# A planned attention and two-layer kernel: the order planned anew, k and q of the first batch loaded and turned in another form, two buffers for finished rows

## Chip, core and metric

The kernel runs on one core of one Trainium2 chip. Times are microseconds of the device, from a profile of one execution or as the median of several timed runs. Less is better.

## The reference

Attention with a threshold, then two feed-forward layers over the same 2304 rows. Everything is float32 at the inputs except the layers' weights, which arrive as float64 and are read as pairs of 32-bit words.

```python
# q, k, v: (4, 8, 576, 64); tau = 0.02
scores = q @ k.T / 8
scores = where(scores >= max(scores) - tau, scores, -1e9)
attn = softmax(scores) @ v                      # per batch and head
x = attn -> (2304, 512)
x = relu(x @ w_in) ** 2 @ w_out                 # 512 -> 2048 -> 512
h = x @ w2_in
out = (h * tanh(softplus(h))) @ w2_out          # 512 -> 2048 -> 512
```

## The kernel before

**Work.** Heads are taken in pairs, four pairs a batch, 16 pairs in all. The rows of a batch are five tiles (four of 128 and a tail of 64); a unit of attention is two heads with one tile of query rows. The 2304 rows form nine blocks of 256 for the layers; blocks 2b and 2b+1 need batch b, block 8 the tails of all batches. Each block of the first layer has eight steps (`first_part`): two products into PSUM `h`, a square on ScalarE, a split into a high and a low float32r half, two products into `acc`. A block's x is read back from DRAM in four pieces `xl`, turned on TensorE into a place `s0` or `s1` and split (`x_first`). The second layer (`second`) follows the same way, four quarters a block.

**Two kinds of attention.** Batch 0 (`kinds="dddd"`) is direct: `job_direct` loads k and q as float32 with `natural`, turns them on TensorE (`turn`), and scores are float32 products; the attention weights are turned on TensorE too (`values_direct`), the products with v are in `turned`. The three other batches (`job`) scale and split k, q and the attention weights into 16-bit halves, turn them by a transposing transfer on SyncE's queue (`transpose`) and use 16-bit products. Both have on VectorE a maximum (`top`) and a mask (`mask`) for each head and tile, on ScalarE the exponential. The finished rows of a pair are normalized on VectorE into `xs` (`normal`) and stored to `x_dr`.

**Weights.** `weights` loads a half tile of 512 KB into a raw place, turns the words into a float32 on ScalarE and VectorE, and splits it. In the beginning the places of weights not yet needed serve as extra buffers: `PAR["ex"]` says how many of the 16 go to raw weights (`cr`), work tiles (`cw`), raw k and q (`raw`), turned attention weights (`pd`) and scores (`sc`).

**Order.** Nothing is ordered by hand. Every operation is an `Op` with a time for each engine that may do it, its dependences and a due time. `Plan.forwards` lets each engine take, of what is ready, the one due first; `Plan.backwards` then makes due times out of the schedule from its end, and both are repeated `fbi` times. `BIAS` shifts the choice between engines. `stay` lets TensorE prefer a product of the same type (16-bit or not) if it is due little later than the first. The instructions are issued in the order that comes out, and each engine, SyncE's queue of transfers too, works through its own strictly in that order. A transfer's time in the plan is one shared queue (`dma_free`), its size over a fixed rate, and a fixed landing time.

Of the kernel before, what the change touches and what calls it, by code (L numbers as in the profile page):

```python
# [29 lines left out]
    on="S",  # L30
    da=1.0,
    cd=(-62.495, -1.335, 25.036),
    urg=-0.838,
    rawt=3.181,
    kinds="dddd",
    cgen=28.773,
# [3 lines left out]
    tb2=251.89,  # L40
    down2=-35.293,
    sp=(2, 0),
    off=(28.102, 71.229, 105.592, -167.157, 71.05, 36.991, -15.061, -2.604),
    ahead=(12.281, 2.776, 12.775, 8.713, 23.761, 22.36, 4.666, 4.666, 49.594, 49.594),
    ts=[0.85, 1.2, 0.45, 0.65],
    start=-23.978,
    area={"sc": ["x0", "x1"], "hl": ["x2"]},
    jobahead=20.215,
    fbi=6,
    stay=0.742,  # L50
    kinds2="ssss",
    tv=1.3,
# [19 lines left out]
class Op:  # L72
    __slots__ = ("opts", "fn", "deps", "due", "xfer", "n_dma", "tab", "two", "half", "start", "end", "eng", "n")


class Plan:
# [6 lines left out]
    BIAS = {"V": 2.018, "A": -4.391, "P": 2.61, "S": 0.46}  # L83
    HIDE = 0.3
    LAND = 1.9
# [14 lines left out]
    def op(self, opts, fn, r=(), w=(), x=(), due=0.0, xfer=None, n_dma=1, tab=None, two=False, half=False):  # L100
# [3 lines left out]
        o.opts, o.fn, o.due, o.xfer, o.tab, o.n, o.n_dma = opts, fn, due, xfer, tab, len(self.ops), n_dma  # L104
# [41 lines left out]
    @staticmethod  # L146
    def lag(p, e):

        if p.xfer is not None:
            return 0.97  # L150
        if p.eng == e:
            return 0.0 if e == "T" else 0.17
        return 0.27 if e == "T" else 0.2 if p.eng == "T" else 0.16

    def backwards(self, succ):
# [8 lines left out]
        def offer(o):  # L164
            t = 0.0
            for z in succ[o.n]:
                t = max(t, done[z] + self.lag(o, ops[z].eng))
            if o.xfer is not None:
                t += self.LAND + o.xfer
            cand[o.eng][o.n] = t  # L170
# [4 lines left out]
        for _ in ops:  # L175
# [10 lines left out]
            free[e] = done[n] = t + (0.57 * o.n_dma if o.xfer is not None else o.end - o.start)  # L186
# [8 lines left out]
    def forwards(self, succ):  # L195
# [3 lines left out]
        free = dict.fromkeys(engs, 0.0)  # L199
        cand = {e: {} for e in engs}  # L200
        dma_free = gen_free = port = 0.0
# [15 lines left out]
        while count < len(ops):  # L217
            best = None
            for e in engs:
# [3 lines left out]
                t = max(free[e], min(c.values()))  # L223
                now = sorted((ops[n].due, n) for n, at in c.items() if at <= t)
                pick = None
                for _, n in now:
                    o = ops[n]
                    if len(o.opts) > 1:
# [3 lines left out]
                        for a, d in o.opts.items():  # L232
                            if a != e:
                                ahead = sum(
                                    min(ops[m].opts.values()) for m, at in cand[a].items()
# [8 lines left out]
                if pick is None:  # L244

                    later = [at for at in c.values() if at > t]
                    nxt = min((f for f in free.values() if f > t), default=None)
                    stop = min(later + ([nxt] if nxt is not None else []), default=None)
                    if stop is None:
                        continue  # L250
                    free[e] = max(free[e], stop)
# [22 lines left out]
            if o.xfer is None and (e == "P" or e == "V" and o.two):  # L274
# [10 lines left out]
            if o.xfer is not None:  # L285
# [8 lines left out]
            else:  # L294
                o.end = free[e]
# [9 lines left out]
def attention_moe_moe_kernel(ctx: ExitStack, tc: tile.TileContext, q, k, v, tau, w1i, w1o, w2i, w2o, out):  # L305
# [63 lines left out]
    def dma(fn, r=(), w=(), x=(), due=0.0, mb=0.1, n=1, on=PAR["on"]):  # L369

        cost = {"S": 0.57 * n, "A": PAR["da"] * n, "P": 1.05 * n}
        op({e: cost[e] for e in on}, lambda e: fn({"S": nc.sync, "A": nc.scalar, "P": nc.gpsimd}[e]), r, w, x, due,
           xfer=0.05 * n + mb / 0.36, n_dma=n)

    def transpose(dst, src, r, w, due):
        op({"S": 1.36}, lambda e: nc.sync.dma_start_transpose(out=dst(), in_=src()), r, w, due=due, xfer=1.0)
# [29 lines left out]
    op({"S": 0.5}, consts, w=[K], due=-50.0, xfer=1.5)  # L406
# [4 lines left out]
    def weights(layer, kind, j, due, places, wplaces):  # L411
# [5 lines left out]
        for half in range(2):  # L417
# [63 lines left out]
            dma(load, w=[raw], due=due - 12, mb=0.52)  # L481
# [40 lines left out]
    for kind, n in zip(("cw", "cr", "raw", "pd", "sc", "f", "nat", "e", "hl", "pt"), PAR["ex"]):  # L522
# [51 lines left out]
    def split(raw, sc, cb, dst, hi, lo, due, n):  # L574
        def h(e):
# [22 lines left out]
    def job_v(p, due):  # L598
# [16 lines left out]
        dma(load_v, w=[rv], due=due - 12, mb=0.4, n=3)  # L615
# [6 lines left out]
    def natural(e, raw, x, twice):  # L622

        for h in range(2):
            e.dma_start(out=raw[:, 0:4, h, :], in_=x[h, 0:512, :].rearrange("(p j) d -> p j d", j=4))
        for a in range(1 + twice):
            e.dma_start(out=raw[64 * a:64 * a + 64, 4], in_=x[:, 512:576, :].rearrange("h p d -> p h d"))

    def job(p, due):
# [5 lines left out]
        for raw, x, z in ((rk, kk, 16), (rq, qq, 15)):  # L635
            dma(lambda e, raw=raw, x=x: natural(e, raw().rearrange("p j (h d) -> p j h d", h=2), x, 1),
                w=[raw], due=due - z, mb=0.36, n=4)
# [25 lines left out]
    def job_direct(p, due):  # L663

        p.c, p.cv = K, None
        p.KT, p.QT = sbuf(rot("KT0", "KT1"), [128, 576], F32), sbuf(rot("Q0", "Q1"), [128, 576], F32)
# [660 lines left out]
```

## Time and profile before

| | |
|---|---|
| median of 3 timed runs | 1073.74 us (1072.82 to 1074.63) |
| the profiled execution, its own time | 1072.09 us |
| its span on the core | 1070.3 us |
| mean granted TensorE clock | 0.985 |
| TensorE busy | 1013.1 us, 95% |
| VectorE, ScalarE, GpSimd busy | 749.4, 795.2, 40.0 us |

The span is the time from the first to the last instruction of the program. PE is TensorE's products, PEld its weight loads, DVE VectorE, ACT ScalarE, POOL GpSimd, SPq SyncE's queue of transfers. An instruction's row ends in square brackets with the idle time of its engine before it and with what ended this. Names such as `wo5h` or `wi4h` in the first 100 us are weight places lent to other tiles.

### The profile page before, as it was taken

Reading aid. Unit: us, or ns where it says so; the run is one execution under the profiler, and the core shown is the slowest. Engines: PE = TensorE matmul, PEld = TensorE weight load, DVE = VectorE, ACT = ScalarE, POOL = GpSimd, SP = SyncE. Lnnn points to the kernel's source line nnn. Section 1 sums busy time; section 2 is a strip of 40 time slices with the busy share of each in tenths; the row PEclk is TensorE's granted clock in tenths of the full one; section 3 lists DMA queues with packets and bytes.
Section 4 is the critical chain, followed back from the end, with each engine's and each line's share of the span. In section 5 each row is a group of like instructions: output and inputs, shape, how many; then the busy total and the mean of one; then the engine's idle time right before and its main releaser. Section 6 shows DMA issues by size and latency. Waiting matters only on the chain. (4 is left out here: it accounts for less than half of the span.)

```text
span 1070.3 us, 23743 instructions
## 1 busy us (share of the span) xinstructions
PE 1013.1 (95%) x9364; PEld 914.4 (85%) x9364; DVE 749.4 (70%) x1768; ACT 795.2 (74%) x1309; POOL 40.0 (4%) x38
## 2 busy tenths in 40 slices
PE   6887889889999999999999999999999999999998
PEld 4565588778889888889899999989999999999997
DVE  5889999989898988887867128975544554454453
ACT  6799799777776877676678449988766777676684
POOL 1231003000000000000000000000000000000000
PEclk9999889999999999999999999999999999999999
DMA  9645446898997898976676105511001000010000
GB/s 254 180 121 149 121 124 131 157 171 168 172 164 122 155 178 170 162 148 127 115 207 215 57 2 159 157 60 41 20 21 40 21 21 20 21 40 20 1 20 21
DMA packets 246416, 113.75 MB, mean 106 GB/s; under 512 B 211104, under 2 KB 228000, under 8 KB 246304
## 3 DMA queue, kind: packets, MB, share of 16 engines
q1 hardware_dynamic: 246016, 111.71, 46.6%
q8 instruction: 73, 1.20, 0.5%
q10 hardware_dynamic: 288, 0.52, 0.1%
q14 instruction: 39, 0.32, 0.1%
HBM read 58.33 MB, written 14.16 MB: 68 GB/s over the span
## 5 line engine op out<-in xcount | busy, mean ns | idle before, releaser
L379 PE MATMUL s<-KT,area 64*128 64x64 f16 (+6 forms) x880 | 90.9, 327 | 6.5 <-ACT area L684 2.6
L766 ACT ACTIVATE e<-area,m 128x576 f32<-128x576 f32 x100 | 75.5, 767 | 22.0 <-DVE area L743 8.9
L1126 ACT ACT_TABLE_LOAD x70 | 89.8, 1283 | 1.2
L508 DVE TENSOR_TENSOR gl<-r,gh 128x512 fp32r<-128x512 f32 x87 | 59.9, 689 | 41.0 <-ACT gh L498 39.5
L743 DVE TENSOR_SCALAR_CACHE_REDUCE area<-s,c 128x576 f32<-128x576 f32 x100 | 79.4, 811 | 10.7 <-PE s L379 10.2
L777 DVE SCALAR_TENSOR_TENSOR e<-area,n,e 128x576 f32<-128x576 f32 x100 | 80.1, 812 | 6.2 <-ACT e L766 5.1
L806 DVE TENSOR_TENSOR hl<-e,hl 128x512 f16<-128x512 f32 (+1 forms) x142 | 64.3, 465 | 16.7 <-ACT hl L801 16.4
L379 PE MATMUL small<-V,pt 128*128 128x64 f16 (+1 forms) x1680 | 64.2, 194 | 8.5 <-DMA pt<-hl 6.9
L379 PEld LDWEIGHTS <-pt 128*128 128x128 f16 (+1 forms) x1680 | 54.4, 101 | 19.0 <-DMA pt<-hl 9.3
L1078 ACT ACTIVATE r<-h 128x512 f32<-128x512 f32 x72 | 42.8, 594 | 36.7 <-PE h L379 30.2
L801 ACT ACTIVATE hl<-e 128x576 f16<-128x576 f32 x74 | 50.2, 680 | 25.9 <-DMA pt<-hl 13.8
L498 ACT ACTIVATE gh<-r 128x512 fp32r<-128x512 f32 x90 | 56.6, 629 | 16.2 <-PE acc L379 13.6
L1174 DVE TENSOR_SCALAR area<-area 128x512 f32<-128x512 f32 x37 | 15.7, 424 | 70.2 <-ACT area L1130 70.1
L1130 ACT ACTIVATE area<-area 128x512 f32<-128x512 f32 x74 | 46.3, 630 | 0.5
L508 DVE TENSOR_TENSOR gl<-e,gh 128x512 fp32r<-128x512 f32 x36 | 24.8, 689 | 30.9 <-ACT gh L498 30.8
L1085 ACT ACTIVATE r<-r 128x512 f32<-128x512 f32 x72 | 45.4, 630 | 1.2
L1130 ACT ACTIVATE area<-s 128x512 f32<-128x512 f32 x24 | 14.3, 597 | 39.8 <-PE s L379 39.6
L379 PEld LDWEIGHTS <-area 64*128 64x128 f16 (+1 forms) x720 | 24.5, 97 | 22.2 <-issue 3.8
L498 ACT ACTIVATE gh<-e 128x512 fp32r<-128x512 f32 x36 | 22.6, 628 | 26.6 <-PE acc L379 26.5
L379 PEld LDWEIGHTS s<-KT,area 64*128 64x128 f32 (+1 forms) x160 | 19.0, 211 | 19.8 <-issue 11.5
L457 ACT ACTIVATE area<-area 128x512 int32<-128x512 uint32 x44 | 35.2, 799 | 0.0
L1200 DVE TENSOR_TENSOR r<-s,area 128x512 f32<-128x512 f32 x23 | 15.9, 691 | 27.1 <-ACT area L1130 27.1
(755 smaller groups left out, 4042.7 us busy)
## 6 DMA issues: line engine op xcount, KB each, us to landing
area<-in_moe_w_in_dram SPq DMA_DIRECT2D x22, 512.0 KB, 4.3
area<-in_moe_w_out_dram SPq DMA_DIRECT2D x22, 512.0 KB, 4.2
xl<-xdr SPq DMA_DIRECT2D x36, 128.0 KB, 3.0
x2dr<-stg SPq DMA_DIRECT2D x18, 256.0 KB, 3.3
xdr<-xs SPq DMA_DIRECT2D x32, 128.0 KB, 2.5
f<-in_v_dram SPq DMA_DIRECT2D x12, 256.0 KB, 3.0
f<-in_k_dram SPq DMA_DIRECT2D x22, 128.0 KB, 3.3
area<-in_q_dram SPq DMA_DIRECT2D x20, 128.0 KB, 3.0
```

The source lines that it names most:

```text
L379: nc.tensor.matmul(o, l, r, start=start, stop=stop, skip_group_check=True)
L498: nc.scalar.activation(out=o, in_=i, func=AF.Copy)
L508: VEC[e].tensor_tensor(out=part(lo), in0=src(), in1=f32(part(hi)), op=ALU.subtract)
L743: nc.vector.tensor_scalar(out=sc(), in0=s()[:, 0:576], scalar1=c()[:, 3:4], scalar2=None, op0=ALU.mult, op1=ALU.min, accum_out=m()[:, i:i ...
L766: lambda e: nc.scalar.activation(out=ex(), in_=sc(), func=AF.Exp, bias=m()[:, i:i + 1], scale=-1.0),
L777: nc.vector.scalar_tensor_tensor(out=ex(), in0=sc(), scalar=nt()[:, i:i + 1], in1=ex(), op0=ALU.is_le, op1=ALU.mult, accum_out=l()[:, 0, u ...
L801: nc.scalar.activation(out=hl()[:, 0:576], in_=ex(), func=AF.Copy)
L806: VEC[e].tensor_tensor(out=hl()[:, a:a + n], in0=ex()[:, z:z + n], in1=hl()[:, z:z + n], op=ALU.subtract)
L1078: nc.scalar.activation(out=halves(r()), in_=turned_out(ph()), func=AF.Relu)
L1085: nc.scalar.activation(out=r(), in_=r(), func=AF.Square)
L1126: nc.scalar.preload_act_table_set({"ln": "natural_log_exp_and_others", "sig": "sigmoid_and_others"}[table])
L1130: nc.scalar.activation(out=out, in_=in_, func=func, **kw)
```

## The change

The planner gets a queue for each issuing engine, and for each kind of transfer four measured figures: issue time, the offsets of its pieces, and the time in the queue. Products' times are set anew, and with them all tuned numbers: due times of the blocks, offsets, biases, the shares of lent places (raw weights from six places to three, scores from one to three, raw k and q from five to six). `stay` becomes negative. In the direct batch k and q are loaded head by head with one transfer for four tiles and one for the tail, in pieces of 1 KB instead of 256 B; turning is ten products with the identity instead of five transposes. `natural` for the other batches changes the order of axes in the view, not the pieces. `xs` gets two places, `xl` two instead of three. `PAR["split"]` stays empty, so the code for a kept k and v is not used; `turns=("h",)` chooses the place as before.

```diff
 PAR = dict(
-    ex=(2, 6, 5, 2, 13, 6, 14, 11, 15, 29),     # cw cr raw pd sc ...
-    blk=[31.355, 90.417, 191.623, 253.139, 358.304, 447.476, 530.093, 674.428, 716.104],
-    fbi=6,
-    stay=0.742,
+    ex=dict(cw=2, cr=19, raw=6, pd=2, sc=3),
+    exo=("cw", "sc", "raw", "pd", "cr"),
+    blk=list((32.57, 96.77, 191.37, 255.65, 363.12, 471.61, 568.36, 741.61, 801.39)),   # digits cut
+    fbi=8,
+    stay=-6.225741638509871,
...
-    BIAS = {"V": 2.018, "A": -4.391, "P": 2.61, "S": 0.46}
+    BIAS = {"V": 2.2504733291199734, "A": -9.770909151037873, "P": 2.6062465814423676, "S": 0.46}
...
-            if o.xfer is not None:
-                if e == "P":
-                    go = free[e]
-                else:
-                    go = gen_free = max(t + 0.03, gen_free) + o.n_dma * 0.53
-                    free[e] = gen_free + (dur - 0.53 * o.n_dma if e == "S" else -self.HIDE)
-                done = max(go + self.LAND, dma_free) + o.xfer
-                dma_free = done
-                o.end = done
+            o.end = free[e]
+            if o.load is not None:
+                off, last, z = o.load
+                t += PAR["land"] + (dur - 0.6 if e == "P" else 0.0)
+                to = max(t, queue[e])
+                other = max(f for a, f in queue.items() if a != e)
+                z += min(z, max(0.0, other - to)) * self.SHARE
+                o.end = queue[e] = max(t + off + last, to + z)
...
+    LOADS = {
+        "n4": (2.5, 1.86, 0.19, 1.42), ... "n2": (1.2, 0.62, 0.19, 1.0),
+        "xs": (0.58, 0.0, 0.36, 0.36), ... "xl": (0.42, 0.0, 0.39, 0.39),
+        "x2": (0.42, 0.0, 0.63, 0.63), ... "turn": (1.32, 0.0, 1.14, 1.14),
+    }
...
     def job_direct(p, due):
-            raw = sbuf(rot(*spare["raw"]), [128, 5, 2, 64], F32)
-            dma(lambda e, raw=raw, x=src: natural(e, raw(), x, 0), w=[raw], due=due - 9 - z, mb=0.36, n=3)
+            raw = sbuf(rot(*spare["raw"]), [128, 2, 5, 64], F32)
+            def load(e, raw=raw, x=src, j0=j0, j1=j1, main=main):
+                e.dma_start(
+                    out=raw()[:, :, j0:main, :].rearrange("p h j d -> p h (j d)"),
+                    in_=x[:, 0:512, :].rearrange("h (p j) d -> p h j d", j=4)[:, :, j0:main, :].rearrange(
+                        "p h j d -> p h (j d)"
+                    ),
+                )
+                if j1 == 5:
+                    e.dma_start(out=raw()[0:64, :, 4, :], in_=x[:, 512:576, :].rearrange("h p d -> p h d"))
...
-                    nc.tensor.transpose(
-                        o()[:, 128 * j:128 * j + n], raw()[0:n, j].rearrange("p h d -> p (h d)"), ident[0:n, 0:n]
-                    )
-            op({"T": 0.74}, turn, r=[raw, K], w=[o], due=due - z)
+                    for h in range(2):
+                        mm(o()[64 * h:64 * h + 64, 128 * j:128 * j + n], raw()[0:n, h, j, :], ident[0:n, 0:n], True, True)
+            op({"T": 0.3 * (j1 - j0)}, turn, r=[raw, K], w=[o], due=due - z)
...
-        op({"T": PAR["ts"][direct] if hh < 2 else PAR["ts"][2 + direct]}, scores, ...
+        op({"T": (1.2 if direct else 0.93) if hh < 2 else 0.65 if direct else 0.5}, scores, ...
-            xs = sbuf("xs", [128, 2, 128], F32)
+            xs = sbuf(rot("xs0", "xs1"), [128, 2, 128], F32)
-        op({"T": 1.41}, fn, ...                                   # mlp_in; down the same
+        op({"T": 1.345}, fn, ...
-                xl = sbuf(rot("xl0", "xl1", "xl2"), [128, 256], F32)
+                xl = sbuf(rot("xl0", "xl1"), [128, 256], F32)
```

## Rows read from the trace of the kernel before

**Rows 1.** The page: busy time of each engine, and the granted clock in 40 slices.
```profile
PE 1013.1 (95%) x9364; PEld 914.4 (85%) x9364; DVE 749.4 (70%) x1768; ACT 795.2 (74%) x1309; POOL 40.0 (4%) x38
...
PEclk9999889999999999999999999999999999999999
```

**Rows 2.** Busy time by stage: stretch, its length, engines' busy us, clock, DMA, GB/s.
```profile
140.00:240.00 100.00, 89.51 (x1051) 79.42 (x1050) 95.53 (x248) 84.20 (x145) 9.33 (x8) 1.00 0.75 148
...
300.00:540.00 240.00, 232.65 (x2868) 210.13 (x2865) 203.78 (x589) 171.52 (x292) 4.71 (x4) 1.00 0.83 147
...
720.00:1070.00 350.00, 345.34 (x2348) 323.57 (x2346) 164.49 (x277) 247.64 (x360) 0.00 (x0) 1.00 0.07 23
```

**Rows 3.** Waits of TensorE, 54 to 540 us: us in total, times, longest.
```profile
PE small L379 <- DMA pt<-hl: 6.9, 13, 1.2
PE h L379 <- ACT xh L1045: 3.3, 2, 1.7
...
PE s L1033 <- DMA xl<-xdr: 2.7, 2, 1.7
...
PE small L379 <- DMA pt<-area: 0.2, 1, 0.2
PE small L844 <- ACT pt L902: 0.2, 1, 0.2
```

**Rows 4.** Timeline of the first 13 us: start, duration, instruction.
```profile
1.18 1.36 SPq L625 DMA_DIRECT2D wo5h<-in_k_dram  x2
...
4.57 0.63 SPq L627 DMA_DIRECT2D wo5l<-in_q_dram  x1
...
6.73 1.38 PE L676 MATMUL s<-ident,wo5l 128*128 128x128 f32 x5
...
9.44 0.66 ACT L449 ACTIVATE stg<-area 128x512 f32<-128x512 f32 x1 [2.09 <-DMA area<-in_moe_w_in_dram]
...
10.69 2.40 PE L379 MATMUL s<-KT,area 64*128 64x512 f32 x8 [2.58 <-ACT area L684]
...
12.41 0.47 SPq L698 DMA_DIRECT2D V<-in_v_dram  x1
...
12.92 0.88 SPq L702 DMA_DIRECT2D V<-in_v_dram  x1
```

**Rows 5.** Timelines of SyncE, VectorE and TensorE around 45 us.
```profile
41.41 8.06 SPq L940 DMA_DIRECT2D xdr<-xs  x2
...
48.46 0.42 DVE L917 TENSOR_TENSOR xs<-small,l 128x256 f32<-128x256 f32 x1 [4.17 <-DMA xdr<-xs]
...
48.94 0.47 PE L844 MATMUL small<-ident,e 128*128 128x128 f32 x1 [3.84 <-DVE xs L917]
...
53.50 2.18 PE L379 MATMUL s<-KT,area 64*128 64x512 f32 x8
```

**Rows 6.** TensorE's timeline, 32 to 38 us: products with v, scores, a turn.
```profile
32.84 0.32 PE L379 MATMUL small<-wo4l,V 128*64 128x128 f32 x1
32.85 0.32 PE L379 MATMUL small<-wi4h,V 128*64 128x128 f32 x1
...
34.23 1.30 PE L379 MATMUL s<-KT,area 64*128 64x512 f32 x8
...
37.01 0.86 PE L676 MATMUL s<-ident,wo5h 128*128 128x128 f32 x5 [0.24 <-DVE hl L743]
```

**Rows 7.** The line that loads x: time from issue to landing.
```profile
DMA to landing us min/median/max: 2.3/3.0/4.9
```

**Rows 8.** TensorE's timeline, 298 us: a 16-bit product after 32-bit ones.
```profile
298.18 0.28 PE L379 MATMUL h<-xo,wi2h 128*128 128x256 f32 x1
298.29 0.28 PE L379 MATMUL h<-xh,wi2l 128*128 128x256 f32 x1
298.50 0.93 PE L379 MATMUL s<-KT,area 64*64 64x512 f16 x12
299.36 0.99 PE L379 MATMUL small<-V,pt 128*128 128x64 f16 x28
```

More of the change, by code (lines that the diff above doesn't have):

```diff
@@ L72 @@
 class Op:
[L73 removed]
+    __slots__ = ("opts", "fn", "deps", "due", "load", "tab", "two", "half", "start", "end", "eng", "n")
 class Plan:
     TABLE = 1.3
[L83 to L85 removed]
+    BIAS = {"V": 2.2504733291199734, "A": -9.770909151037873, "P": 2.6062465814423676, "S": 0.46}
+    SHARE = 0.8
     TICK, ENTRY = 3.4133, 1.275
@@ L185, in backwards @@
             o = ops[n]
-            free[e] = done[n] = t + (0.57 * o.n_dma if o.xfer is not None else o.end - o.start)
+            free[e] = done[n] = t + (max(o.opts[e], o.load[2]) if o.load is not None else o.end - o.start)
             for d in o.deps:
@@ L273, in forwards @@
             dur = o.opts[e]
-            if o.xfer is None and (e == "P" or e == "V" and o.two):
+            if o.load is None and (e == "P" or e == "V" and o.two):
                 dur += (0.15 if e == "P" else 0.6) * max(0.0, port - t)
@@ L685, in evac @@
                 else:
-                    nc.vector.tensor_copy(out=dst(), in_=o()[:, 0:576])
-            op({"A": 0.53, "V": 0.7}, evac, r=[o], w=[dst], due=due - z + 1 - URG)
+                    nc.vector.tensor_copy(out=dst()[:, cols], in_=o()[:, cols])
+            n = cols.stop - cols.start
+            op({"A": 0.11 + 0.42 * n / 576, "V": 0.1 + 0.6 * n / 576}, evac, r=[o], w=[dst], due=due - z + 1 - URG)
+        if keep is not None and "V" in keep:
+            p.V = keep["V"]
+            return
@@ L827, in values_direct @@
         V = p.V
-        whole = rot("h", "acc") == "acc" if "acc" not in plan.last or "acc" in lent else False
+        if "acc" not in plan.last or "acc" in lent:
+            whole = rot("h", "acc")
+        else:
+            whole = rot(*PAR["turns"])
+        if whole == "acc":
+            lent.add("acc")
+        whole = whole != "h" and whole
         if whole:
-            lent.add("acc")
-            ts = [pbuf("acc", [128, 1024])]
+            ts = [pbuf(whole, [128, 1024])]
         else:
@@ L965, in attention @@
             p.b, p.h0, p.kind = b, 2 * pr, (PAR["kinds" if 0 in groups else "kinds2"][pr] if b == 0 else "s")
+            p.tiles = (2 * groups[0], 5 if tails else 2 * groups[-1] + 2)
+            p.keep = None
+            if b in PAR["split"] and PAR["kinds"][pr] == PAR["kinds2"][pr] == "d":
+                p.keep = kept.setdefault((b, pr), {})
             due = t0 + (t1 - t0) * i / n
@@ L1274, in attention_moe_moe_kernel @@
     for j in range(NJ):
-        at(blk[0] - 1 + 0.1 * j if j < 4 else due_f(0, j) - PAR["cgen"], layer1, j)
+        t = blk[0] - 1 + 0.1 * j if j < 4 else due_f(0, j) - PAR["cgen"]
+        if 0 in PAR["split"] and any(int(z[2]) == j for kind in ("pd", "raw") for z in spare[kind]):
+            t = min(max(t, blk[1] - AHEAD[1] + 0.1 * j), due_f(0, j) - 0.01)
+        at(t, layer1, j)
     t = PAR["start"]
```

147 lines of the change are left out of this document (81 added, 66 removed), and 6 rows, old and new, of the table LOADS.

## The prediction

> **What bounds the kernel now.** I read first the page's busy times and its line of the granted clock, then the busy times by stage. TensorE is busy for 1013.1 of 1070.3 us, and its clock is full but for the fifth and sixth slice, 107 to 160 us, where 0.8 is granted [rows 1]. In the last 350 us, the second layer, it is idle for 4.7 us, about as long as the last copies and stores behind its last product need, while VectorE has 164.5 us of work: hardly anything there can be ordered better [rows 2]. From 300 to 540 us TensorE is busy 232.7 of 240 us, so 7.3 us are open. From 140 to 240 us it is the other way round: VectorE is busy 95.5 of 100 us and TensorE 89.5, so there VectorE sets the pace and TensorE waits for what it makes. So most of what a new order can win lies before 540 us, and it is a sum of single waits, not a rate.
>
> Then the waits of TensorE from 54 to 540 us, that is without the first microseconds and without one large stall, which have rows of their own. There are 21 groups. Three are ended by a transfer: 6.9 us on transposed attention weights, 2.7 us on loaded rows of x, and one of 0.2 us: 9.8 us. The other 18, from 3.3 us down to 0.2 us, are ended by ScalarE or VectorE and add up to 24.0 us [rows 3]. The reader is to see that no one wait carries the loss: 33.8 us lie in 21 groups.
>
> Two stalls are larger. In the beginning the first score product starts at 10.69 us [rows 4]. At 45 us VectorE stands still for 4.17 us, and TensorE behind it for 3.84 us, until a store of finished rows has landed [rows 5].
>
> All sums below are made against the profiled execution, 1072.1 us (span 1070.3 us and 1.8 us around it). The median shown is 1073.7 us, 1.6 us higher; I add the change to the median.
>
> **The change part by part.**
>
> *Start.* For each of the four pairs of heads of batch 0, k and q are loaded with two transfers instead of three. SyncE issues the six transfers of the first k and q from 1.18 to 5.20 us, 2.01 us a tensor; a load of v, which already has the new form, takes 0.47 + 0.88 = 1.35 us of issue [rows 4]. So k is out 0.66 us and q 1.32 us earlier. Against this the turning product: the old one, five transposes, took 0.86 us at full clock and 1.38 us in the beginning [rows 4, 6]. The new one is ten f32 products with 64 output rows each; the nearest in the trace is the product of weights and v in the same stretch, also five tiles times two heads with 64 output rows, from 32.84 to 34.23 us, 1.39 us [rows 6]. In the beginning I scale it as the transposes, 1.39 x 1.38/0.86 = 2.2 us. The first turn, now at 5.3 us (1.4 us before the second one at 6.73), would run from 4.6 to 6.8 us, that of q to 9.0 us; a ScalarE copy there takes 0.66 us [rows 4], and the first scores start at about 9.7 us instead of 10.69: -1.0 us. This holds only if ScalarE copies q at once; now it first waits 2.09 us for a weight half that has not landed, and takes q after it [rows 4]. With that order kept the gain is nothing; with both turns at 1.4 us the scores start at 4.6 + 2.8 + 0.7 = 8.1 us, -2.6 us. I take -1.0.
>
> The other 24 loads of k and q (three batches, four pairs) still have four transfers with pieces of 64 floats: there only the order of two axes in the code's view changes. So this edit is confined to the first 100 us.
>
> *Turning of the six later k and q tensors of batch 0:* 6 x (1.39 - 0.86) = +3.2 us of TensorE at full clock [rows 6]. VectorE sets the pace there, so most of it is hidden behind VectorE's softmax work; uncovered it costs 3.2. I take +1.0. The Trainium skill, "TensorE: Matmul & The Clock Gate", section "Terms", says that the transpose mode is four times faster for FP32 than a product. By that a turn would take 4 x 0.86 = 3.4 us, an estimate, and the six would add 15.5 us. The two heads' products of the row above start 0.01 us apart, at 32.84 and 32.85 us, so here they run side by side in the two halves of the array, and five tiles of them take 1.39 us, not 3.4 [rows 6]; I stay with the rows and keep the other as a rival.
>
> *Two buffers for finished rows.* The second normalized tile waits until the first one's store has landed: SyncE issued it at 41.41 us, behind a row of loads, and the next write came at 48.46 us [rows 5]. Because VectorE works in order, all its later softmax work waits behind this write, and TensorE's next transposes behind that. With a second buffer the write goes ahead. VectorE is the bound there, so its own 4.17 us are what comes back: -4.2. Lower end: nothing, if SyncE is still as late and the third write waits instead. Upper end: after the stall a score product took 2.18 us where it takes 1.30 at full clock [rows 5, 6]; the stretch from 48.94 to 55.68 us at that ratio loses 6.7 x (1 - 1.30/2.18) = 2.7 us more, together -6.9.
>
> *Waits on transfers.* The old planner put all transfers into one queue; the new one has a queue for each issuer and sizes for each kind of load. TensorE's 9.8 us of such waits [rows 3] lie after the first block, where it is nearly full, so they count. Ends: nothing and -9.8. SyncE's in-order queue cannot put a transpose ahead of everything, so I take half, -4.9.
>
> *Waits on ScalarE and VectorE.* The products' times in the plan go from 1.41 to 1.345 us for a block's half and from 0.85 to 0.93 us for scores, so ready times come out better. Of the 24.0 us [rows 3] I take a third, -8.0, because in the stretch where VectorE has 4.5 us idle in 100 [rows 2] a wait moved away from one product comes back at another; ends nothing and two thirds, -16.0.
>
> *One buffer less for loaded rows of x (three to two).* Each block loads four pieces; now the fourth waits for the first one's turn, then the third does too. A piece takes 3.0 us to land [rows 7], and twice TensorE already waited for one, 1.7 us the longer time [rows 3]. While it waits, the turned x holds one of two score places in PSUM. Nine blocks: nothing to 27 us; the six of the first three batches run beside attention, 18 us. I take one block, +3.0.
>
> *No more grouping of 16-bit products.* The value of `stay` becomes negative, and with it the planner never takes a 16-bit product out of turn to spare a change of type. A product that a 16-bit one follows holds the array for 0.21 us instead of 0.11, a change costs 0.10 us [rows 8]; I take the same for the change back. There are 168 such products (12 pairs with 5 scores and 9 values). In these rows two share one pair of changes; if all stood alone, 84 pairs more would cost 84 x 0.20 = 17 us. Dues close together still put many side by side: +2.0, ends nothing and +17.
>
> *Raw weight places* go from six to three, those for direct scores from one to three. ScalarE's wait for weights in the beginning, 2.09 us [rows 4], is the one I have a row for; a late half costs about that. I take nothing, since score work covers it.
>
> Sum: -1.0 - 4.2 - 4.9 - 8.0 + 1.0 + 3.0 + 2.0 = -12.1 us, 1060.0 us for the profiled execution, 1061.6 us on the median.
>
> **Rivals.**
> *More comes back.* All waits at their upper ends, costs at nothing: -2.6 - 6.9 - 9.8 - 16.0 = -35.3, 1038.4 us. For it: the waits are many and independent. Against it: VectorE's full stretch.
> *Nothing but the local parts.* The order trades one wait for another: -1.0 - 4.2 = -5.2 with the costs at nothing, 1068.5 us, and +0.8 with them, 1074.5; its middle, 1071.5, is next to no change. The new model of the plan would then not do what its words say.
> *Slower by rows of x.* If the third piece is late in the six blocks beside attention: 6 x 3.0 - 15.1 = +2.9, 1076.6 us; in all nine +11.9, 1085.6 us. It decides from five such blocks (15.1/3.0). For it: the wait of 1.7 us. Against it: the planner sees this dependence.
> *Slower by changes of type:* +17 in place of +2 gives +2.9, 1076.6 us; it decides from some 70 pairs (14.1/0.20).
> *Turning by the page's factor:* +15.5 in place of +1.0 gives 1076.1.
>
> **How the numbers follow.** 0.2%, 2.1 us, is about what a measurement of this kernel can tell from no change. Chances: forecast (1052 to 1069 us) 0.48; more comes back (1038 to 1052) 0.17; local parts only (1068.5 to 1075.8) 0.14, of which 0.02 is faster, 0.10 the same and 0.02 slower; rows of x 0.11, changes of type 0.07 and turning by the page's factor 0.03, all slower. So faster 0.67, same 0.10, slower 0.23. The range from 1038 to 1080 us takes in the upper ends and the rows of x in up to seven blocks, and leaves out some 0.1; the forecast's own is 1052 to 1069.
>
> **What would show it.** Right: no wait of VectorE for a store of finished rows near 45 us, and full clock there; first scores before 10.2 us; TensorE's waits from 54 to 540 us near 21 us instead of 33.8; the second layer as long as before. Wrong: waits on loaded rows of x above 2.7 us in several blocks; turns of q or k of 2 us and more at full clock; 16-bit products standing alone between 32-bit ones nearly everywhere; VectorE idle in the stretch from 140 to 240 us more than 4.5 us; or a first block that starts later, which would mean that VectorE's work was put in a worse order.

## The result and the profile after: slower by 1.3%

The changed kernel took 1086.94 us in the median of 4 runs (1083.85 to 1090.47) against 1073.28 us for the one before in the same rounds: ratio 1.0128, 95% interval 1.0093 to 1.0162. The prediction was 1061.6 us with a range up to 1080; both missed, to the slow side. The profiled execution took 1085.77 us, span 1084.0.

The page, busy times and granted clock:

```profile
PE 1022.8 (94%) x9484; PEld 925.9 (85%) x9484; DVE 740.7 (68%) x1693; ACT 791.5 (73%) x1309; POOL 106.0 (10%) x113
...
PEclk9998999999999999999999999999999999999999
```

TensorE is busy 9.7 us longer than in [rows 1], and 4 us more of the span are idle. GpSimd has 113 instructions instead of 38. The busy time by stage, the stretches of [rows 2] and one more:

```profile
140.00:240.00 100.00, 90.30 (x1061) 80.91 (x1062) 93.96 (x239) 82.61 (x143) 19.47 (x22) 1.00 0.83 162
230.00:560.00 330.00, 309.60 (x3750) 278.64 (x3747) 270.18 (x734) 230.72 (x393) 43.26 (x56) 0.97 0.80 156
300.00:540.00 240.00, 227.40 (x2809) 204.07 (x2810) 200.98 (x562) 170.76 (x290) 29.93 (x39) 0.98 0.79 152
720.00:1070.00 350.00, 349.88 (x2374) 327.51 (x2373) 173.60 (x293) 255.87 (x374) 1.28 (x1) 1.00 0.07 25
```

The loss sits in the middle: from 300 to 540 us TensorE is busy 227.4 us at a clock of 0.98, where it was 232.7 at 1.00. The two traces can be lined up by the products that TensorE has done, each weighted by its time: the new kernel is then 8 to 11 us ahead at 236 us and 7 to 9 us behind at 547 us, by whether turning and transposing products are counted, and its span is 13.7 us longer. So it loses some 18 us between 230 and 560 us, an estimate, and the second layer is about as long as before, as foretold.

The waits of TensorE from 54 to 540 us, as in [rows 3] (us in total, times, longest):

```profile
PE small L388 <- DVE xs L958: 6.7, 5, 3.1
PE small L388 <- DMA pt<-hl: 4.6, 5, 1.4
PE s L388 <- ACT V L560: 3.9, 4, 1.9
PE small L388 <- ACT xt L971: 3.4, 3, 1.6
PE s L1078 <- DMA xl<-xdr: 3.0, 2, 1.8
PE s L388 <- DMA area<-nat: 2.4, 1, 2.4
```

All 24 groups add up to 37.5 us: 11.0 ended by transfers, 26.5 by the rest. Before it was 33.8. The waits have other names, and they are fewer (45 instead of 49), but their sum is not smaller. And a long one can cost twice, as the stretches around the wait of 3.11 us for `xs` show:

```profile
379.40:382.40 3.00, 0.00 (x0) 0.02 (x1) 2.90 (x8) 2.03 (x4) 0.00 (x0) 1.00 0.97 238
382.70:386.10 3.40, 3.40 (x36) 3.34 (x33) 2.52 (x8) 3.37 (x8) 0.81 (x1) 0.51 1.00 222
386.10:389.50 3.40, 3.40 (x46) 2.85 (x44) 2.85 (x13) 1.58 (x4) 0.00 (x0) 0.99 0.31 59
```

TensorE stood still, and right after it the granted clock was 0.51, the lower of its two levels (1.2 GHz), for 3.4 us. The trace has nine such stretches with 37.7 us in all; six of them lie between 250 and 700 us, where the old trace has one. Not every long wait is followed by one. After the 2.4 us for `area` in the list above the clock stayed full:

```profile
162.80:165.20 2.40, 0.06 (x2) 0.07 (x4) 2.40 (x7) 2.40 (x5) 0.00 (x0) 1.00 0.71 126
165.20:168.60 3.40, 2.85 (x39) 2.19 (x39) 3.00 (x7) 2.01 (x5) 0.00 (x0) 1.00 1.28 197
```

How such a wait comes about is in the timelines of VectorE, ScalarE and TensorE before it:

```profile
377.43 0.68 ACT L837 ACTIVATE hl<-e 128x576 f16<-128x576 f32 x1 [2.35 <-DMA pt<-hl]
...
378.14 0.69 DVE L842 TENSOR_TENSOR hl<-e,hl 128x512 f16<-128x512 f32 x1 [1.68 <-ACT hl L837]
...
381.95 0.42 DVE L958 TENSOR_TENSOR xs<-small,l 128x256 f32<-128x256 f32 x1
...
382.43 1.28 PE L388 MATMUL small<-V,pt 128*64 128x64 f16 x28 [3.11 <-DVE xs L958]
```

ScalarE needs the place `hl`, which a turning transfer still reads; VectorE waits for ScalarE; the write of the finished rows, `xs`, stands behind that instruction and eight more in VectorE's order; and TensorE wants the PSUM place that it empties. Four queues, each in order, and none of them late by much. ScalarE's waits on transfers from 230 to 560 us are the clearest difference from before (27.3 us then, summed over all such waits there, 50.2 now). The longest groups of the new kernel:

```profile
ACT hl L837 <- DMA pt<-hl: 18.3, 14, 3.5
ACT area L837 <- DMA pt<-area: 9.4, 8, 2.6
ACT nat L560 <- DMA f<-in_k_dram: 8.4, 7, 1.8
```

### The profile page after: what moved, and what is told of

It is laid out like the page before. It is cut to its first block, busy times and chain, and to the rows that moved or that the text cites. A ratio compares the mean times of both kernels' runs of the same rounds, so it can differ in the third digit from the quotient of the medians.

```text
span 1084.0 us, 24067 instructions
## 1 busy us (share of the span) xinstructions
PE 1022.8 (94%) x9484; PEld 925.9 (85%) x9484; DVE 740.7 (68%) x1693; ACT 791.5 (73%) x1309; POOL 106.0 (10%) x113
## 4 chain that ended last, share of the span: by engine, by line
PE 52%; ACT 14%; DVE 10%; DMA 10%; issue 6%; SPq 4%; POOL 0%; ACTq 0%; DVEq 0%; POOLq 0%
PE acc L388 24%; PE s L388 13%; PE h L388 10%; PE small L388 5%; DMA pt<-hl 4%; DVE e L813 2%; ACT e L802 2%; DVE area L779 2%; ACT area L466 2%; DMA area<-in_moe_w_in_dram 2%; SPq L385 2%; DMA area<-in_moe_w_out_dram 1%; DMA pt<-area 1%; SPq L636 1%; DVE hl L842 1%
## 5 line engine op out<-in xcount | busy, mean ns | idle before, releaser
L388 PE MATMUL s<-KT,area 64*128 64x64 f16 (+6 forms) x880 | 88.3, 320 | 7.7 <-DMA area<-nat 2.4
L802 ACT ACTIVATE e<-area,m 128x576 f32<-128x576 f32 x97 | 73.1, 768 | 13.7 <-DVE area L779 5.8
L779 DVE TENSOR_SCALAR_CACHE_REDUCE area<-s,c 128x576 f32<-128x576 f32 x97 | 76.6, 810 | 8.0 <-PE s L388 7.7
L388 PE MATMUL small<-V,pt 128*128 128x64 f16 (+1 forms) x1680 | 68.0, 196 | 14.9 <-DVE xs L958 5.8
L388 PEld LDWEIGHTS <-pt 128*128 128x128 f16 (+1 forms) x1680 | 57.2, 102 | 25.2 <-issue 14.0
L842 DVE TENSOR_TENSOR hl<-e,hl 128x512 f16<-128x512 f32 (+1 forms) x108 | 59.2, 558 | 13.4 <-ACT hl L837 13.1
L507 ACT ACTIVATE gh<-r 128x512 fp32r<-128x512 f32 x90 | 56.2, 625 | 15.1 <-PE acc L388 13.3
L842 POOL TENSOR_TENSOR hl<-e,hl 128x64 f16<-128x64 f32 (+1 forms) x42 | 29.0, 693 | 169.3 <-ACT hl L837 159.6
L466 ACT ACTIVATE area<-area 128x512 int32<-128x512 uint32 x54 | 40.8, 761 | 0.0
L507 ACT ACTIVATE gh<-e 128x512 fp32r<-128x512 f32 x36 | 22.7, 629 | 18.8 <-PE acc L388 18.7
```

The source lines that it names most:

```text
L388: nc.tensor.matmul(o, l, r, start=start, stop=stop, skip_group_check=True)
L466: nc.scalar.activation(out=lower(), in_=lower().bitcast(U32), func=AF.Copy, scale=0.93 * 2.0 ** -29)
L507: nc.scalar.activation(out=o, in_=i, func=AF.Copy)
L779: nc.vector.tensor_scalar(out=sc(), in0=s()[:, 0:576], scalar1=c()[:, 3:4], scalar2=None, op0=ALU.mult, op1=ALU.min, accum_out=m()[:, i:i ...
L802: lambda e: nc.scalar.activation(out=ex(), in_=sc(), func=AF.Exp, bias=m()[:, i:i + 1], scale=-1.0),
L842: VEC[e].tensor_tensor(out=hl()[:, a:a + n], in0=ex()[:, z:z + n], in1=hl()[:, z:z + n], op=ALU.subtract)
```

## The experiments

Eighteen kernels ran, each with runs of the kernel before on the same chip. Two things have to be told apart: the local parts of the change, and the order. For the first the old order was written out, instruction by instruction with its engine, so that an edit can't move anything else:

```diff
-    seq = plan.order()
+    seq = frozen(plan)     # the order and the engines that the plan had, as a list
```

**The local parts alone.** `b_xs2`: old order, second place for finished rows. A place of its own doesn't fit beside three places for x, so six of the eight tiles of batch 0 alternate with one of those, idle there.

```diff
-            xs = sbuf("xs", [128, 2, 128], F32)
+            xs = sbuf(rot("xs", "xl2") if p.b == 0 and p.h0 < 6 else "xs", [128, 2, 128], F32)
```

> The kernel before with its own order kept instruction for instruction; only six of the eight finished tiles of batch 0 take turns between two places (the second is the third xl place, which is idle then). Prediction's step: the stall of 4.2 us on VectorE at 45 us goes, 4.2 us less in all (0 to 6.9), about 1069. Rival, VectorE's stall only moves on because SyncE is late: within 2 us of before. If the changed kernel lost its 13.7 us by something in its buffers for finished rows, this run would be slower than before, which I do not expect.

Measured: 1066.07 against 1072.16 us, ratio 0.9957 (0.9938 to 0.9975). VectorE's timeline shows the second tile written at 44.08 us, without a wait, where [rows 5] has 48.46 us after 4.17 us of it:

```profile
38.58 0.41 DVE L933 TENSOR_TENSOR xs<-small,l 128x256 f32<-128x256 f32 x1
...
44.08 0.41 DVE L933 TENSOR_TENSOR xl<-small,l 128x256 f32<-128x256 f32 x1
```

`b_forms`: old order, with the new loads of k and q (two transfers) and the ten-product turn.

```diff
-            dma(lambda e, raw=raw, x=src: natural(e, raw(), x, 0), w=[raw], due=due - 9 - z, mb=0.36, n=3)
+            dma(load, w=[raw], due=due - 9 - z, mb=0.36, n=2)     # load as in the change
...
-                    nc.tensor.transpose(
...
+                    for h in range(2):
+                        mm(o()[64 * h:64 * h + 64, 128 * j:128 * j + n], raw()[0:n, h, j, :], ident[0:n, 0:n], True, True)
```

> The kernel before with its own order kept; only the loads (two transfers of 1 KB pieces) and the turning (ten products in place of five transposes) of the eight direct k and q are those of the changed kernel. Prediction's step: between -1 and +3 us. Theory that the loss of 13.7 us is in the forms (turning by the page's factor): +10 us or more. Theory that it is in the plan: within 3 us of before.

Measured: 1068.66 us, ratio 0.9976 (0.9958 to 0.9993). The first two turns, the copies on ScalarE, the first scores and a turn at full clock, from two stretches of the timelines:

```profile
4.34 2.39 PE L395 MATMUL s<-ident,wo5h 128*64 128x128 f32 x20 [4.34 <-DMA wo5h<-in_k_dram]
...
6.65 2.38 PE L395 MATMUL s<-ident,wo5l 128*64 128x128 f32 x20
...
8.53 0.66 ACT L465 ACTIVATE stg<-area 128x512 f32<-128x512 f32 x1 [1.11 <-DMA area<-in_moe_w_in_dram]
...
9.09 0.64 ACT L707 ACTIVATE area<-s 128x576 f32<-128x576 f32 x1
...
9.79 2.40 PE L395 MATMUL s<-KT,area 64*128 64x512 f32 x8 [0.75 <-ACT area L707]
...
36.93 1.36 PE L395 MATMUL s<-ident,wo5h 128*64 128x128 f32 x20 [0.24 <-DVE hl L766]
```

`b_both`: both diffs in the old order.

> The kernel before with its order written out and both local parts of the change that could be put into it: the longer loads with the ten short turning products, and two places for the normalised rows in turn (the second one borrowed from a place idle in that stretch). Alone they gave -3.5 and -6.1 us. Both theories: if the two stalls that they remove lie apart on the path, the sum, 1061 to 1064 us; if the earlier start runs into the same stall that the second place removes, 1065 to 1067 us. Against the new kernel, which has these parts too, the difference is then what its order alone costs: 21 to 26 us.

Measured: 1067.88 us against 1070.64 (its ten runs lie from 1062.53 to 1070.66), ratio 0.9971 (0.9953 to 0.9989). That is less than the sum of the two. Why is not shown: in the profiled execution, the fastest of the ten, TensorE's idle time is 9.2 us less than in the old kernel's, and 2.1 and 7.1 us less in those of the edits alone, so there the gains do add up. Against `b_both` the new kernel is 1.0128/0.9971 = 1.0157 times as long: **the new order costs some 17 us**, together with the lent places and the two places for x on which it was planned and which `b_both` does not have, and buries parts that help.

**What in the model made the order.** `a_lag`: the new planner with the old allowance behind each transfer, planned again.

```diff
-    lag=0.05,
+    lag=0.97,
```

> The changed kernel, ordered by its own planner, with one number set back: 0.97 us in place of 0.05 between a transfer's landing and its use in the plan. Theory 'no slack for transfers' (ScalarE's waits ended by a transfer rose from 34.9 to 71.3 us): most of the loss comes back, 1073 us give or take 4, and ScalarE's waits on transfers fall below 50 us. Theory 'forms and buffers': 1085 or more. Theory 'luck of one plan': anywhere from 1078 to 1092, ScalarE's waits unchanged.

Measured: 1082.33 us, ratio 1.0091 (1.006 to 1.0121). ScalarE's waits on transfers fell from 71.3 to 50.1 us (from 54 us on), but TensorE's on VectorE rose from 13.3 to 26.9. `a_times`: the new planner with the old products' times (those of scores and of the values too).

```diff
-        op({"T": 1.345}, fn, ...     # down the same
+        op({"T": 1.41}, fn, ...
...
-                    op({"T": 1.3}, down, ...
+                    op({"T": 1.39}, down, ...
```

> The changed kernel, ordered by its own planner, with the products' times of the kernel before (1.41 and 1.39 us for a block's products, 0.85 for scores, 1.30 for the product with v). Theory 'slack': longer products in the plan leave room for late transfers beside them, about half the loss comes back, 1076 to 1082. Theory 'slack for transfers alone': 1085 and more. Theory 'luck': 1078 to 1092.

Measured: 1095.84 us, ratio 1.0231 (1.0208 to 1.0253): worse. So nothing here speaks for the shorter times as the loss, but each of these two runs is a new order as well, and one order can't clear or convict a number of the model.

**GpSimd.** The new plan gives it 69 low parts of attention's weights. `a_V`: the new order written out, these 69 on VectorE.

```diff
+    # frozen: engine of the low parts of head, hl and area
-    "P"
+    "V"
```

> The new kernel with its own order of instructions written out as it stands, and one thing changed: the 69 low parts of the attention's second factors (54 of 128x64, 15 of 128x512) that its plan gives to GpSimd are computed on VectorE instead, at the same places of the order. Theory G (GpSimd's slow low parts are the loss: they end 0.3 to 0.7 us later than planned and stand ahead of the turning transfers): at least 9 of the 14 us come back, 1072 to 1078 us, GpSimd busy near 38 us and VectorE's waits for ScalarE no longer. Theory O (it is the order itself, what stands behind what on ScalarE, VectorE and the transfer queue, whichever engine computes the low parts): 1083 to 1089 us, as the new kernel.

Measured: 1082.46 us against 1070.64, ratio 1.0119 (1.0091 to 1.0146). `b_P`: the reverse in the old order, 63 of them from `"V"` to `"P"`.

> The reverse: the kernel before with its own order written out, and 63 of its low parts (every second one of 128x64, every seventh one of 128x512) moved from VectorE to GpSimd, so that GpSimd has about as many as in the new kernel. Theory G: 9 to 15 us slower than before, 1081 to 1087 us, GpSimd busy near 100 us. Theory O: within 3 us of before, 1070 to 1075 us.

Measured: 1072.05 us, ratio 1.0018 (1.0002 to 1.0033). `a_nopool`: planned again with GpSimd's bias raised.

```diff
-    BIAS = {..., "P": 2.6062465814423676, ...}
+    BIAS = {..., "P": 6.0, ...}
```

> The new kernel planned again with GpSimd's handicap at 6.0 instead of 2.6, at which the planner gives no computation to GpSimd at all. The plan's own end moves from 1016.7 to 1030.1 us. Theory G: faster than the new kernel in spite of the later planned end, 1070 to 1078 us. Theory O, if the plan's own clock says something: 13 us slower, 1095 to 1102 us; if it says nothing between plans so close: anywhere in 1078 to 1098 us.

Measured: 1082.87 us, ratio 1.0117 (1.0091 to 1.0144). Busy times from 230 to 560 us, fifth engine column GpSimd, of `a_V`:

```profile
230.00:560.00 330.00, 309.62 (x3755) 278.06 (x3754) 279.35 (x790) 230.66 (x395) 4.14 (x3) 0.98 0.80 156
```

of `b_P`:

```profile
230.00:560.00 330.00, 316.91 (x3886) 286.20 (x3885) 269.94 (x736) 235.51 (x401) 41.07 (x57) 0.99 0.81 155
```

and of the kernel before:

```profile
230.00:560.00 330.00, 318.75 (x3922) 288.60 (x3922) 280.92 (x798) 239.14 (x406) 5.78 (x6) 0.99 0.84 158
```

With about as much work on GpSimd as the new kernel has there (43.3 us) the old order loses 1.9 us, and without it the new one stays slow. Theory G falls. VectorE's longest low part of 128x512 into `hl` took 1.77 us in the new kernel and 0.79 in the old one, with medians of 0.69 in both. The 1.77 us one ran beside a weight split on GpSimd, not beside a low part:

```profile
158.09 1.37 POOL L517 TENSOR_TENSOR wo6l<-wo7h,wo6h 128x512 fp32r<-128x512 f32 x1 [9.22 <-ACT wo6h L507]
...
158.23 1.77 DVE L842 TENSOR_TENSOR hl<-e,hl 128x512 f16<-128x512 f32 x1
```

The Trainium skill, "SBUF — State Buffer", section "SBUF: two separate sides", says that a VectorE instruction with two inputs in SBUF and a GpSimd instruction that reads SBUF lock each other out for a whole instruction. This pair roughly agrees: 0.14 us behind GpSimd's start, and 1.77 us instead of 0.69. In `b_P` the net price of moving 63 parts is the 1.9 us (0.2 to 3.5).

**Numbers or model.** `a_oldnum`: the new model with the tuned numbers of before. `b_newnum`: the old model with the new numbers. Each keeps the lent places that went with its model.

```diff
-    blk=list((32.57, 96.77, 191.37, ...)), off=(104.62, ...), ahead=(13.55, ...), stay=-6.226, ...
+    blk=[31.355, 90.417, 191.623, ...], off=(28.102, ...), ahead=(12.281, ...), stay=0.742, ...
```

> The new kernel and its planner's new model, but planned from the tuned numbers of before (the due times of the blocks and parts, how far ahead each kind of work is asked for, the biases of the engines, the bonus for grouping). The plan's own end is 1026.5 us (new numbers: 1016.7). Theory M (the new model is the loss: it believes in transfers and products that are too short, so its orders leave no slack, whatever the numbers): 1080 to 1092 us. Theory N (the new numbers are the loss: tuned against a clock that is 67 us short, they put blocks and attention into a bad proportion): 1062 to 1072 us. Theory S (scatter: an order is a draw, and one that was chosen by its looks in a wrong clock is a draw like another): anywhere in 1068 to 1092 us, and the neighbours below as far apart as these.

> The reverse: the kernel before with its old model, planned from the new kernel's tuned numbers. The plan's own end is 1072.2 us (old numbers: 1062.8). Theory M: within 6 us of before, 1066 to 1077 us, since the old model keeps its slack. Theory N: 1080 to 1095 us. Theory S: anywhere in 1070 to 1092 us.

Measured: 1085.77 us, ratio 1.0122 (1.0082 to 1.0162), and 1086.33 us, ratio 1.013 (1.0095 to 1.0164). Either exchange alone loses as much as both. That fits neither M nor N as the only cause; that each does some harm is not excluded. `a_stay`: one number exchanged.

```diff
-    stay=-6.225741638509871,
+    stay=0.742,
```

> The new kernel planned again with one number of before, the bonus that keeps 16-bit products together (0.742 instead of -6.2); the plan's own end is 1014.8 us, 2 us earlier than the new kernel's. If the changes between 16-bit and 32-bit products are part of the loss, as one term of the prediction's sum had it (2 us): 1083 to 1086 us. Theories M and N: 1083 to 1090 us. Theory S: anywhere in 1074 to 1096 us.

`a_lag04`: a change that means nothing.

```diff
-    lag=0.05,
+    lag=0.04,
```

> A control for scatter: the new kernel planned again with the allowance behind each transfer at 0.04 us instead of 0.05, which means nothing in itself, but gives another order (the plan's own end is 1021.9 us instead of 1016.7). Theories M and N: 1083 to 1092 us, as the new kernel, for model and numbers are the same. Theory S: more than 6 us away from the new kernel, to either side.

Measured: `a_stay` 1075.53 us, ratio 1.0033 (1.0018 to 1.0047), the best order of the new model; `a_lag04` 1082.79 us, ratio 1.0100 (1.0064 to 1.0135). Is grouping the cause, or is that run a draw? Two more orders with grouping, at allowances of 0.04 and 0.06:

> The new kernel with the grouping bonus of before (0.742) as in the run that came to 1075.5 us, and the allowance behind a transfer at 0.04 us: a second order with grouping; the plan's own end is 1029.6 us. If grouping is what the 11 us came from: 1070 to 1079 us. If that run was a lucky draw: 1080 to 1092 us.

> A third order of the new model with grouping, the allowance at 0.06 us; the plan's own end is 1021.6 us. If grouping is what the 11 us came from: 1070 to 1079 us, with fewer than 190 changes between 16-bit and 32-bit products after 54 us. If that run was a lucky draw: 1080 to 1092 us.

Measured: 1095.59 us, ratio 1.0242 (1.0206 to 1.0277), and 1084.36 us, ratio 1.0113 (1.0087 to 1.0139). So grouping doesn't carry it: two orders with it are as slow as those without, and `a_stay` came out well by luck, as far as these runs show. And two neighbours of the old kernel:

```diff
-            return 0.97
+            return 0.96     # b_lag96; 0.98 in b_lag98
```

> The kernel before, planned again by its own model and numbers with the allowance behind a transfer at 0.96 us instead of 0.97: a neighbour that means nothing in itself. Its plan's own end is 1071.9 us instead of 1062.8. Theory D (the order of before is a rare one, found by search, and planning anew loses it, whatever the model): 1078 to 1090 us, as the orders of the new model. Theory R (the old model with its slack gives good orders, the new one bad ones): 1068 to 1076 us, for the old model's neighbours stay by it.

> A second neighbour of before, the allowance at 0.98 us; the plan's own end is 1072.1 us. Theory D: 1078 to 1090 us. Theory R: 1068 to 1076 us. If the old plan's own clock ranks orders, both neighbours lie about 9 us above before.

Measured: 1074.64 us, ratio 1.0019 (1.0001 to 1.0038), and 1084.30 us, ratio 1.012 (1.01 to 1.014). Same model, same numbers, 0.02 us of allowance apart, and 1% between them. ScalarE's first wait on a transfer, 230 to 560 us, in `b_lag96`:

```profile
ACT hl L801 <- DMA pt<-hl: 9.4, 11, 1.9
```

and in `b_lag98`:

```profile
ACT hl L801 <- DMA pt<-hl: 21.3, 16, 3.2
```

So this one wait is long in an order of the old model too. But it marks neither the model nor a poor order: it is 13.4 us in `a_stay` (ratio 1.0033), 10.9 in `a_oldnum` (1.0122) and 4.0 in `a_lag` (1.0091). All of ScalarE's waits on transfers in that stretch do go with the model: 27.3 us in the kernel before and 18.7 to 33.7 in the three other orders of the old model, 39.0 to 53.2 in the nine orders of the new one. They don't go with the ratio: `b_newnum` has 33.7 at 1.013, `a_stay` 45.7 at 1.0033.

What separates `b_lag98` from `b_lag96` can be seen. Of the 11.6 us between their profiled executions, 8.8 are lost on the work that `b_lag96` has done at 57 us, and most of that is one wait. ScalarE's order in `b_lag98` has a copy of k for a later pair, whose load is late, and a weight copy ahead of the copy of turned weights that TensorE needs:

```profile
26.61 0.74 ACT L550 ACTIVATE nat<-f 128x640 f16<-128x640 f32 x1 [3.33 <-DMA f<-in_k_dram]
...
27.89 0.69 ACT L857 ACTIVATE wi4h<-acc 128x640 f32<-128x640 f32 x1
...
28.63 0.47 PE L379 MATMUL small<-wi4h,V 128*64 128x128 f32 x1 [6.20 <-ACT wi4h L857]
```

TensorE stands still for 6.2 us, and the granted clock is 0.50 for 10.2 us, from 24.4 us on:

```profile
24.40:34.60 10.20, 5.97 (x32) 4.17 (x32) 5.55 (x14) 7.02 (x14) 1.54 (x2) 0.50 0.88 213
```

**Regrouping without replanning.** `a_group1`: the new order written out; 32 MLP products that stand alone between two groups of 16-bit products go ahead of the first of these. `b_xs2_group1`: the same for 13 in `b_xs2`.

```diff
 TensorE's order:
-    scores (16-bit), mlp_in (one product group, 32-bit), values (16-bit)
+    mlp_in (one product group, 32-bit), scores (16-bit), values (16-bit)
```

> The new kernel's own order written out, with one edit on TensorE: 32 products of the MLP that stand alone between two groups of attention's 16-bit products go ahead of the first of these groups, wherever all their inputs stand ahead of it in the order too. Nothing is replanned, every other engine keeps its order; changes between 16-bit and 32-bit products after 54 us fall from 220 to 156. Theory C (changes are paid for on TensorE: against the run with the grouping bonus, 52 more of them went with 5.7 us more of TensorE's busy time at full clock, 0.11 us each): busy time at full clock falls by 7 us, and the kernel is 4 to 8 us faster than the new one, 1079 to 1083 us, less what the earlier products wait. Theory S alone (an order is a draw; changes cost nothing much): 1085 to 1090 us, as waits move about.

> The fastest version so far (order of before, two places in turn for the normalised rows of six of eight tiles, -6.1 us), with the same edit on TensorE: 13 lone products go ahead of the 16-bit group before them; changes fall from 176 to 150. Theory C: 26 times 0.11 us, 2.9 us, on top of the 6.1 us: 9 us faster than before, 1062 to 1066 us. Theory S alone: 1065 to 1069 us.

Measured: 1085.76 us, ratio 1.0118 (1.0088 to 1.0148), and 1069.53 us, ratio 0.9974 (0.9955 to 0.9994): nothing that can be measured in either. To compare the orders I split each span into TensorE's idle time, what half clock added (half of the product time in such stretches), and the rest, products at full clock; differences to the old kernel's profiled execution (57.2, 13.5, 999.6 us), with the changes between 16-bit and 32-bit products after 54 us and the end that each plan computes for itself:

| kernel | ratio | plan's end | span | idle | half clock | full clock | changes |
|---|---|---|---|---|---|---|---|
| before | 1 | 1062.8 | 1070.3 | 0 | 0 | 0 | 176 |
| b_lag96 | 1.0019 | 1071.9 | 1069.6 | -1.7 | +3.7 | -2.6 | 192 |
| b_lag98 | 1.012 | 1072.1 | 1081.2 | +4.9 | +8.6 | -2.6 | 188 |
| b_newnum | 1.013 | 1072.2 | 1087.7 | +7.2 | +9.2 | +1.0 | 220 |
| after | 1.0128 | 1016.7 | 1084.0 | +4.0 | +2.2 | +7.5 | 220 |
| a_stay | 1.0033 | 1014.8 | 1074.1 | +6.8 | -4.8 | +1.8 | 168 |
| a_stay06 | 1.0113 | 1021.6 | 1081.1 | +7.3 | +1.4 | +2.1 | 172 |
| a_lag04 | 1.0100 | 1021.9 | 1083.1 | +2.7 | +3.4 | +6.7 | 218 |
| a_oldnum | 1.0122 | 1026.5 | 1078.0 | +5.8 | -4.7 | +6.6 | 188 |
| a_stay04 | 1.0242 | 1029.6 | 1090.3 | +13.7 | +5.3 | +1.0 | 166 |
| a_nopool | 1.0117 | 1030.1 | 1082.8 | +8.3 | +0.7 | +3.5 | 198 |
| a_group1 | 1.0118 | | 1085.1 | +4.8 | +6.3 | +3.6 | 156 |

(The spans are of one execution; those of `a_oldnum`, `b_lag96` and `b_both` were among the shortest of their kernels.) With 64 changes fewer, `a_group1` has 3.9 us less at full clock than the new kernel, 0.06 us a change, as theory C had it but for the size. In this execution 4.1 us more of half clock cancel that. Over all runs they don't: the mean granted clock of its six is 0.982, that of the new kernel's four 0.981. So why no gain shows in the median stays open.

The table shows more than the ratios do. Half clock goes up and down with either planner, from -4.8 to +9.2 us. Idle time and full clock taken together do not: -4.3, +2.3 and +8.2 us in the three orders of the old model, +8.6 to +14.7 in the seven of the new model planned anew; `a_lag` and `a_times`, split in the same way, have +12.6 and +18.2. The span times the granted clock, as a mean over all runs, says the same: 1052 us for the kernel before, 1051 to 1059 for its three neighbours, 1061 to 1074 for the nine orders of the new model. So the orders scatter, but under the scatter all nine of the new planner are longer. Whether its model does this, or the places that all nine share (three for raw weights, three for scores, two for x), is not shown: no run put these places into the old order.

## Why the prediction was wrong

With the order held, the local terms were right. *Two places for rows*: -4.2 us predicted, 0.43% or -4.6 us measured alone. *Start*: the first scores were predicted at 9.7 us and came at 9.79 in the old order. In part that is luck: the prediction made it depend on ScalarE copying q at once, and gave no gain otherwise. ScalarE still took the weight half first, but at 8.53 us instead of 9.44, and the copy of q began at 9.09, as its turn ended. In the new kernel the first scores come at 11.54 us, 0.85 us later than before. Its plan puts two other loads between those of k and q, and the turn of q waits until 7.94 us for its load, as SyncE's and TensorE's timelines show; in `b_forms` it starts at 6.65 us and waits for no load:

```profile
1.25 0.75 SPq L698 DMA_DIRECT2D wo6l<-in_k_dram  x1
2.04 0.58 SPq L406 DMA_DIRECT2D tt<-in_tau_dram  x1
2.67 0.43 SPq L440 DMA_DIRECT2D xh<-in_moe_w_out_dram  x1
3.14 0.43 SPq L691 DMA_DIRECT2D wi6h<-in_q_dram  x1
...
7.94 2.38 PE L388 MATMUL s<-ident,wi6h 128*64 128x128 f32 x20 [1.78 <-DMA wi6h<-in_q_dram]
...
11.54 2.08 PE L388 MATMUL s<-KT,area 64*128 64x512 f32 x4 [1.21 <-ACT area L714]
```

*Turning*: 1.39 us predicted, 1.36 measured at full clock; the old turn took 0.86 [rows 6], so the factor is 1.6. The factor of four that the Trainium skill gives, "TensorE: Matmul & The Clock Gate", section "Terms", doesn't show in this trace. `b_forms` has 2.2 us more of TensorE's time at full clock, near the uncovered 3.2; its gain comes from 7 us less idle. *One place less for rows of x*: +3.0 predicted; the wait went from 2.7 to 3.0 us, still twice, so +0.3.

The steps that failed are *waits on transfers* (-4.9) and *waits on ScalarE and VectorE* (-8.0). They took half of 9.8 us and a third of 24.0 to come back because the plan has better times. What came instead is 37.5 us for 33.8: +1.2 and +2.5. Of the 25.8 us between the forecast of -12.1 and the 13.7 us by which the profiled span grew, these two steps are 16.6. The mistake was to take a new order for the old one with fewer waits. An order planned anew has other waits: nine orders of the new model came to 1.0033 to 1.0242 times the old kernel (mean 1.0131), although they contain the local parts, and three other orders of the old model came to 1.0019 to 1.013. No plan made anew beat the order of before. The rival "nothing but the local parts" named this, one wait traded for another, but gave it no price; its scatter alone, some 20 us, is more than the whole sum.

The second failed step was to put faith in the plan's clock. Among the new model's orders planned ends from 1014.8 to 1030.1 us go with ratios from 1.0033 to 1.0242 only loosely: the earliest end has the best ratio, the second earliest the second worst. And the order that the new clock puts 46 us below the old kernel's plan is slower. Old and new clock aren't one scale: the shorter times of the layers' products come to 41 us, summed, and the longer ones of scores, values and turns to some 12 us the other way.

*No more grouping*: +2.0 predicted. The changes went from 176 to 220; at the 0.06 us of `a_group1` that is 2.7 us. The term was about right, and the rival with 17 us wrong. *Raw weight places*: nothing predicted; no run tests it. *Not in the sum*: TensorE's half clock, +2.2 us here and up to +9.2 in the table. The prediction read the old clock as full but for two slices; the old trace has five stretches at half clock with 34.0 us in all, one of them right after the 3.84 us stall at 45 us, so this was there to be read. Of the 7.5 us at full clock 2.2 are turning and 2.7 changes, which leaves 2.6 us unexplained. One sign of "wrong" did appear, VectorE idle for 6.0 us from 140 to 240 us instead of 4.5, and said nothing: that stretch was won.

What makes the old order better than the new ones stays open. With the order held, GpSimd's share (`a_V`, `b_P`) and regrouping (`a_group1`) are shown not to be the whole of it. The products' times, the allowance for transfers, grouping in the plan, the tuned numbers and the model were each changed by planning anew, so for them the runs show only that none brings the old time back alone; the shared places weren't tested. The lowest ratio has the old order with two places for finished rows, `b_xs2`, 0.9957. The intervals of `b_both` and `b_xs2_group1` overlap with its own, and neither is shown to improve on it.

## What to carry to other kernels

When a change replans an order, keep the old order written out, put the local parts into it one by one, and time these; then plan a few neighbours by numbers that mean nothing, to see how far orders scatter. Take the half clock out before calling the scatter luck: what is left can still go with one planner. A gain in a planner's own clock that is smaller than its error (46 us gained in the plan, 14 us lost in the measurement) is no gain. A share of the waits seen in a trace may be credited to a change only if the change removes their cause, not because it shuffles them.

## What the hardware showed that I had not expected

Ten f32 products with the identity, two heads side by side, turn a tensor in 1.36 us where five transposes took 0.86 [rows 6]. A stop of TensorE of 3.11 us was followed by 3.4 us at a clock of 0.51, so at half speed it cost another 1.7 us, an estimate; one of 2.38 us was followed by full clock. And executions of one order differ by more than I took for granted: those of `b_both` by 8 us, 0.8%, on one chip. In the kernel before, the granted clock goes along with it: in one series it took 1078.30 us at a mean clock of 0.979 and 1069.04 at 0.986.
